# A list-scheduled kernel gets a new order, three new constants in its planner, and two units of q whose exponentials run row by row

## The chip, the cores and the metric

One Trainium2 chip, one core. The metric is the device time of one execution in microseconds (us), as the median of repeated runs. A profiled execution, recorded separately, gives the rows shown below.

## The reference

Three layers follow one another, all in float32. Linear attention comes first (4 batches, 8 heads, 576 positions, 64 columns): a softmax of q over its columns, a softmax of k over the positions, and `q_s @ (k_s^T @ v)`. Its result, 2304 x 512, passes through a SwiGLU layer and then a bilinear one.

```python
q_s = np.exp(q - q.max(-1)); q_s /= q_s.sum(-1) + 1e-9      # row by row
k_s = np.exp(k - k.max(2));  k_s /= k_s.sum(2) + 1e-9       # column by column
x = einsum('bhsd,bhde->bhse', q_s, einsum('bhsd,bhse->bhde', k_s, v))
x = (silu(x @ w_gate) * (x @ w_val)) @ w_out                # 512 -> 1536 -> 512
x = (x @ w_a) * (x @ w_b) @ w_out2                          # 512 -> 1536 -> 512
```

## The kernel before, in words

**Precision.** Each operand of the large products is split into a high part and a low part (float32r), and a product is three passes of TensorE: low by high, high by low, high by high. Cutting the operands apart is work of VectorE, ScalarE and GpSimd. The weights arrive in a wide format of two 32-bit words per number, and are converted first: for a tile of w_gate, w_val and w_out (`convert`, lines 367 to 452) the steps are an absolute value (L421 on ScalarE or L423 on VectorE), a scaling of the low words (L426, ScalarE), two clamps and shifts (L428, L431, VectorE), a merge of signs (L437, VectorE), an addition of the low words (L442, VectorE or GpSimd), the high part (L447, ScalarE) and the low part (L331, the helper `pair`, VectorE or GpSimd). Tile f of layer 1 is called `w_f`; a tile has 1536 columns, and from tile 4 on it comes in two halves of 768.

**Stages.** The attention of a batch has four units of two heads (`attend`, from L536). A unit takes its largest k (`tm`, `kx`, `kr`, `kb`), the exponentials, `kv` (L745), the normalised and transposed q (`qt`, `ql`), and at the end `xt` and `xl` (L809, L819), whose result for batch 0 is split into `xhl`, the input of the first up products. A unit's buffers are called `ut` (units of batches 0 and 1). Then block 0 of layer 1 runs over twelve weight tiles: products `u_0_f` (L860 for f = 0, L875 later), gate and product on ScalarE and VectorE (`s`, L886, L889), splitting into `h`, and down products `acc` (L902) of the tile before. Block 1 does the same, with the attention of batches 2 and 3 between its products. From about 265 us on, the rest of layer 1 and the whole of layer 2 run as 18 steps of a Strassen-like scheme (products `p`, `q`, `o`, from L1154), with sums and splits (`raww`, `l2w`, `temps`, `latewr`) on VectorE, ScalarE and GpSimd.

**What sets the order.** Every operation is given to a `Plan` (L31) with its engine, an estimated cost, what it reads and writes, and for some of them a second engine that could do it. `Plan.prepare` works out a due time for each, backwards from the products; `emit` adds the corrections of the table `MOVES` (number of the operation, shift in us) and `order` then simulates the engines and picks, again and again, the ready operation of earliest due time. The instructions are issued in that order: each engine's queue is fixed when the kernel is built, and an engine that waits holds back all that stands behind it. The constants `HOP`, `FROM_TENSOR`, `DMA_RATE` and `DMA_END` exist only in this simulation; on the chip they matter by the order that comes out.

**The q exponentials.** In the units of batch 0 GpSimd subtracts a row's maximum from q (L709, L713), one ACTIVATE takes the exponential of k and q together (1280 columns, L717), and VectorE adds up the rows (L768). In the units of the other batches the maximum is given as the bias of nine ACTIVATEs on ScalarE, one for each row group, which also return the row's sum (L728); k has its own exponential of 640 columns (L721). The tuple `BYROW` names the units of batch 0 that take the second way; before it is empty.

Of the kernel before, what the change touches and what calls it, by code (L numbers as in the profile page):

```python
# [30 lines left out]
class Plan:  # L31
# [10 lines left out]
    SAME, HOP, TO_TENSOR, TO_GPSIMD, FROM_TENSOR = 0.033, 0.1, 0.055, 0.1, 0.2  # L42
    OVER = dict(vector=0.08, scalar=0.1, gpsimd=0.045)
    PORT = 0.08
    SLACK = 0.7
    DMA_START, DMA_END, DMA_RATE, DMA_LANES = 1.0, 1.45, 330e3, 8
# [25 lines left out]
    def add(self, engine, cost, fn, reads=(), writes=(), due=None, after=(), table=None, nbytes=0, other=None,  # L72
# [3 lines left out]
        for access, write in [(a, False) for a in reads] + [(a, True) for a in writes]:  # L76
# [14 lines left out]
            for key, (last, readers) in buf.seen.items():  # L91
                if part is None or key is None or key == part:
                    if last is not None:
                        deps.add(last)
                    if write:
                        deps.update(readers)
# [1295 lines left out]
```

## Time and profile before

| | |
|---|---|
| median of 3 runs | 938.73 us (938.71 to 941.14) |
| the profiled execution | 938.23 us |
| its span, first to last instruction | 936.4 us |
| TensorE busy | 901.8 us, 96% of the span |
| VectorE, ScalarE, GpSimd busy | 69%, 57%, 37% |
| DMA | 121.45 MB, 130 GB/s over the span |

A busy TensorE is one with a matmul under way; matmuls overlap, so that the mean duration of one in a list is longer than the step from one to the next. The profiled execution lies 0.5 us below the median of the runs, and its span 1.8 us below its own time.

### The profile page before, as it was taken

Reading aid. Unit: us, or ns where it says so; the run is one execution under the profiler, and the core shown is the slowest. Engines: PE = TensorE matmul, PEld = TensorE weight load, DVE = VectorE, ACT = ScalarE, POOL = GpSimd, SP = SyncE. Lnnn points to the kernel's source line nnn. Section 1 sums busy time; section 2 is a strip of 40 time slices with the busy share of each in tenths; the row PEclk is TensorE's granted clock in tenths of the full one; section 3 lists DMA queues with packets and bytes.
Section 4 is the critical chain, followed back from the end, with each engine's and each line's share of the span. In section 5 each row is a group of like instructions: output and inputs, shape, how many; then the busy total and the mean of one; then the engine's idle time right before and its main releaser. Section 6 shows DMA issues by size and latency. Waiting matters only on the chain.

```text
span 936.4 us, 13123 instructions
## 1 busy us (share of the span) xinstructions
PE 901.8 (96%) x4560; PEld 742.4 (79%) x4560; DVE 646.6 (69%) x1025; ACT 529.4 (57%) x1027; POOL 347.5 (37%) x324
## 2 busy tenths in 40 slices
PE   5599999999999999999999999999999999999998
PEld 3377777777787888888887888888878888788886
DVE  7899996553498898676778778765686444454444
ACT  4999987868566665555462556443543453333310
POOL 6523212112063233444574534662765213242210
PEclk9999999999999999999999999999999999999999
DMA  9968874453437455454413664422032210110003
GB/s 270 292 215 245 274 231 157 136 179 110 115 108 239 138 164 186 143 155 128 132 57 101 214 203 122 122 84 67 23 98 84 79 46 23 45 45 23 23 1 113
DMA packets 108154, 121.45 MB, mean 130 GB/s; under 512 B 31928, under 2 KB 83896, under 8 KB 107960
## 3 DMA queue, kind: packets, MB, share of 16 engines
q1 hardware_dynamic: 102424, 116.55, 40.0%
q10 hardware_dynamic: 5664, 4.07, 1.3%
q8 instruction: 36, 0.59, 0.3%
q14 instruction: 30, 0.25, 0.1%
HBM read 88.60 MB, written 31.98 MB: 129 GB/s over the span
## 4 chain that ended last, share of the span: by engine, by line
PE 78%; DVE 12%; DMA 4%; issue 2%; ACT 1%; SPq 1%; DVEq 0%; ACTq 0%
PE p L1154 33%; PE o L1264 15%; PE u L875 8%; PE q L1238 7%; PE o L1266 6%; PE acc L902 4%; PE o L1273 2%; DVE a L437 2%; DVE w L331 1%; DVE a L442 1%; DVE l2w L331 1%; DVE a L428 1%; PE xt L809 1%; DVE a L431 1%; DMA latewr<-in_moe_w_out_dram 1%
## 5 line engine op out<-in xcount | busy, mean ns | idle before, releaser
L1154 PE MATMUL p<-l2w,l2w 128*128 128x512 f32 x1512 | 353.1, 390 | 1.6 <-DVE temps L331 1.6
L1154 PEld LDWEIGHTS p<-l2w,l2w 128*128 128x128 f32 x1512 | 282.8, 188 | 62.1 <-DVE temps L331 2.9
L875 PE MATMUL u<-xhl,w 128*128 128x512 f32 x552 | 142.5, 405 | 4.9 <-POOL w L331 2.8
L331 POOL TENSOR_TENSOR l2w<-raww,l2w 128x512 fp32r<-128x512 f32 x71 | 106.0, 1496 | 87.1 <-ACT l2w L338 84.7
L338 ACT CAST l2w<-raww 128x512 fp32r<-128x512 f32 x144 | 88.2, 621 | 81.9 <-PE p L1154 37.7
L875 PEld LDWEIGHTS u<-xhl,w 128*128 128x128 f32 x552 | 101.4, 191 | 29.5 <-DVE w L331 4.8
L331 DVE TENSOR_TENSOR sums<-o,sums 128x512 f32<-128x512 f32 x120 | 82.4, 688 | 53.6 <-PE o L1264 40.7
L331 DVE TENSOR_TENSOR temps<-p,temps 128x512 f32<-128x512 f32 x90 | 61.9, 688 | 54.0 <-PE p L1154 52.7
L1264 PE MATMUL o<-l2w,hp 128*128 128x512 f32 x288 | 97.0, 391 | 0.9 <-DVE sums L331 0.9
L331 DVE TENSOR_TENSOR l2w<-raww,l2w 128x512 fp32r<-128x512 f32 x73 | 57.5, 799 | 29.9 <-ACT l2w L338 29.8
L1166 ACT COPY temps<-p 128x512 f32<-128x512 f32 x72 | 42.1, 586 | 60.6 <-PE p L1154 58.6
L902 PE MATMUL acc<-h,w 128*128 128x512 f32 x288 | 73.0, 399 | 0.0
L507 POOL TENSOR_TENSOR latewr<-latewr 128x512 uint32<-128x512 uint32 x23 | 33.0, 1437 | 93.1 <-DVE latewr L502 87.1
L1238 PE MATMUL q<-rest,l2w 128*128 128x256 f32 x432 | 65.4, 283 | 0.0
L1264 PE MATMUL o<-l2w 128*128 128x512 f32 x192 | 64.4, 389 | 0.0
L1264 PEld LDWEIGHTS o<-l2w,hp 128*128 128x128 f32 x288 | 53.3, 188 | 13.3 <-DVE sums L331 2.8
L902 PEld LDWEIGHTS acc<-h,w 128*128 128x128 f32 x288 | 53.1, 188 | 12.4 <-issue 1.4
L1238 PEld LDWEIGHTS q<-rest,l2w 128*128 128x128 f32 x432 | 58.6, 192 | 0.9
L331 POOL TENSOR_TENSOR raww<-raww,spare 128x512 f32<-128x512 f32 x12 | 17.3, 1442 | 89.1 <-DVE l2w L331 88.9
L1266 PE MATMUL o<-hp,l2w 128*128 128x512 f32 x144 | 48.7, 392 | 1.1 <-DVE sums L331 1.1
L1264 PE MATMUL o<-l2w,l2w 128*128 128x512 f32 x168 | 49.7, 390 | 0.0
L1266 PE MATMUL o<-l2w 128*128 128x512 f32 x144 | 48.3, 390 | 0.0
(192 smaller groups left out, 1463.3 us busy)
## 6 DMA issues: line engine op xcount, KB each, us to landing
raww<-wf SPq DMA_DIRECT2D x36, 512.0 KB, 3.8
raww<-wf SPq DMA_DIRECT2D x36, 256.0 KB, 3.2
wf<-latewr SPq DMA_DIRECT2D x36, 256.0 KB, 3.4
wf<-a SPq DMA_DIRECT2D x16, 384.0 KB, 2.7
latewr<-in_moe_w_a_dram SPq DMA_DIRECT2D x24, 256.0 KB, 4.2
latewr<-in_moe_w_b_dram SPq DMA_DIRECT2D x24, 256.0 KB, 3.1
latewr<-in_moe_w_out_dram SPq DMA_DIRECT2D x12, 512.0 KB, 5.1
wr<-in_moe_w_gate_dram SPq DMA_DIRECT2D x22, 256.0 KB, 4.0
```

Source lines behind the costliest of these rows:

```text
L331: engine.tensor_tensor(out=out(), in0=x(), in1=y(), op=op)
L338: add("scalar", act_us(n), lambda: nc.scalar.copy(out=hi(), in_=src()), src_keys, [hi_key])
L437: add("vector", dve_us(e), lambda rows=rows, halves=halves: nc.vector.scalar_tensor_tensor(out=a(halves), in0=rows()[..., 1], scalar=0xC00 ...
L507: engine.tensor_tensor(out=u32(), in0=u32(), in1=r()[..., 0], op=ALU.add)
L875: nc.tensor.matmul(ps()[:, 0:n], lhsT=wv[:, c, :], rhs=x()[:, xs, c, 0:n], start=(a == 0 and c == 0), stop=(a == 2 and c == KD - 1))
L902: nc.tensor.matmul(ps()[:, 0:n], lhsT=w()[:, 4 + ws, o * P:(o + 1) * P], rhs=h()[:, hs, 0:n], start=begin, stop=end)
L1154: nc.tensor.matmul(ps()[:, 0:width], lhsT=wv(o)[:, m, ws, c, :], rhs=ops_x[o][xs][1]().rearrange("p (c n) -> p c n", c=2)[:, c, 0:width], ...
L1166: add("scalar", act_us(n), lambda: nc.scalar.copy(out=to[1]()[:, 0:n], in_=ps()[:, 0:n]), [ps], [to[0]], due=main["at"] + main["soon"])
L1238: nc.tensor.matmul(ps[m]()[:, 0:256], lhsT=wv(o)[:, m, ws, c % 2, :], rhs=rest_x[xs][1]().rearrange("p (c n) -> p c n", c=KD)[:, c, :], st ...
L1264: nc.tensor.matmul(ps(), lhsT=lhs(i, hs), rhs=outs_w[i][1]()[:, ws * 512:(ws + 1) * 512], **ends)
L1266: nc.tensor.matmul(ps()[:, 0:width], lhsT=outs_w[i][1]()[:, ws * 512 + r * P:ws * 512 + (r + 1) * P], rhs=hs2[i][t][1]()[:, hs * 512:hs * ...
L1273: nc.tensor.matmul(ps()[:, o * 256:(o + 1) * 256], lhsT=outs_w[i][1]()[:, ws * 512 + at:ws * 512 + at + P], rhs=rest_h[1]()[:, (2 * i + hs ...
```

## The change

Four constants or rules of the simulation are new: the rate of the DMA queues is taken as 345 KB/us (330 before), the landing as 1.4 us (1.45); a place that a matmul only read counts as free 0.04 us before that product's end (`READ_BY_TENSOR`), where 0.2 us was added before for any dependency on TensorE; and a slot is free 0.033 us after its last user (0.1 before). `MOVES` is a wholly new table. `BYROW` becomes (1, 3): two of the four units of batch 0 take their exponentials of q row by row.

```diff
+    READ_BY_TENSOR = -0.04
...
-    DMA_START, DMA_END, DMA_RATE, DMA_LANES = 1.0, 1.45, 330e3, 8
+    DMA_START, DMA_END, DMA_RATE, DMA_LANES = 1.0, 1.4, 345e3, 8
...
-        27, 38.5, 35, -20.2, 47, -5.8, 52, -11.1, 53, 7.6, 79, -9.5, 88, -3.9, 93, -18.9, 100, -28.2, 119,
...
+        3, 17.6, 6, 34.4, 8, 13, 9, 39.6, 39, 18.8, 44, 21.6, 53, -48.3, 57, 2.5, 60, 29.3, 70, -26.4, 71,
...
                     if last is not None:
                         deps.add(last)
+                        made.add(last)
...
-    def hop(self, first, then):
+    def hop(self, first, then, made=True):
 
         if first == "tensor":
-            return 0.0 if then == "tensor" else self.FROM_TENSOR
+            return 0.0 if then == "tensor" else self.FROM_TENSOR if made else self.READ_BY_TENSOR
...
-            return max(end[u] for u in users) + self.HOP if all(u in end for u in users) else self.FAR
+            if not all(u in end for u in users):
+                return self.FAR
+            return max(end[u] + (self.READ_BY_TENSOR if ops[u]["engine"] == "tensor" else self.SAME) for u in users)
...
-    BYROW = ()
+    BYROW = (1,3)
```

The file grows by nine lines: L331 of before is L340 after it, L442 is L451, L860 is L869.

**TensorE, start of the SwiGLU layer.** Before, all four units of batch 0 are finished when the first products `u_0_0` begin, and between them and those of tile 1 (`u_0_1`) stand the first products of a unit of batch 1 (`kx_483`, `kb_496`):

```order
L860 MATMUL u_0_0_0_410<-xhl_0_304,w_0_347 128x512 x3
L860 MATMUL u_0_0_1_420<-xhl_0_304,w_0_347 128x512 x3
L680 MATMUL kx_483<-ident,tm_477 128x128 x2
L680 MATMUL kx_483<-ident,ut_425 128x128
L685 MATMUL kb_496<-ident,kr_492 128x128
L875 MATMUL u_0_1_0_513<-xhl_0_304,w_1_475 128x512 x12
L875 MATMUL u_0_1_1_557<-xhl_0_304,w_1_475 128x512 x12
L902 MATMUL acc_0_581<-h_0_0_508,w_0_347 128x512 x3
```

Now the first chunk of `u_0_0` stands ahead of the end of the third unit (`ut_103`) and the fourth (`ut_106`), and nothing stands between `u_0_0` and `u_0_1`:

```order
L805 MATMUL qt_367<-ident,ut_103 128x128 x4
L869 MATMUL u_0_0_0_376<-xhl_0_339,w_0_254 128x512 x3
L808 MATMUL ql_397<-ident_87,ut_103 128x64
L818 MATMUL xt_400<-ut_103 128x512
L828 MATMUL xl_412<-ut_103 128x64
L869 MATMUL u_0_0_1_415<-xhl_0_339,w_0_254 128x512 x3
L869 MATMUL u_0_0_0_376<-xhl_0_339,w_0_254 128x512 x3
L869 MATMUL u_0_0_1_415<-xhl_0_339,w_0_254 128x512 x3
L805 MATMUL qt_432<-ident,ut_106 128x128 x4
L869 MATMUL u_0_0_0_376<-xhl_0_339,w_0_254 128x512 x3
```

The first products of batch 1 have moved behind `u_0_1`, into the down products.

**VectorE, weight tile 1.** Before, the two last splits of `xhl` and the chain of tile 1 (`a_1`) end with the addition L442, and the split of `w_1` is not in this queue:

```order
L442 ISA a_0_1_255<-wr_0_1_169,a_0_1_255 128x1024
L331 TENSOR_TENSOR xhl_0_304<-xt_388,xhl_0_304 128x512
L428 TENSOR_SCALAR a_1_0_402<-a_1_0_402 128x1536
L331 TENSOR_TENSOR xhl_0_304<-xt_398,xhl_0_304 128x512
L431 TENSOR_SCALAR a_1_0_402<-a_1_0_402 128x1536
L437 SCALAR_TENSOR_TENSOR a_1_0_402<-wr_1_223,a_1_0_402 128x1536
L428 TENSOR_SCALAR a_0_2_456<-a_0_2_456 128x512
L442 ISA a_1_0_402<-wr_1_223,a_1_0_402 128x3072
L431 TENSOR_SCALAR a_0_2_456<-a_0_2_456 128x512
```

Now the chain is followed by the last of `xhl`, three steps of tile 0's third part (`a_0_2`) and the split of `w_1` itself:

```order
L340 TENSOR_TENSOR xhl_0_339<-xt_400,xhl_0_339 128x512
L446 SCALAR_TENSOR_TENSOR a_1_0_381<-wr_1_223,a_1_0_381 128x1536
L451 ISA a_1_0_381<-wr_1_223,a_1_0_381 128x3072
L340 TENSOR_TENSOR xhl_0_339<-xt_453,xhl_0_339 128x512
L437 TENSOR_SCALAR a_0_2_441<-a_0_2_441 128x512
L440 TENSOR_SCALAR a_0_2_441<-a_0_2_441 128x512
L446 SCALAR_TENSOR_TENSOR a_0_2_441<-wr_0_2_215,a_0_2_441 128x512
L340 TENSOR_TENSOR w_1_463<-a_1_0_381,w_1_463 128x2x3x256
L711 TENSOR_REDUCE st_491<-ut_429 128x8
```

The split of `w_1` came to this queue, with the absolute value of the tile ahead of it (it was on ScalarE).

**GpSimd, the same place.** Before, the addition L442 for `a_0_2` and then the split of `w_1`:

```order
L660 MEMSET ut_425 64x64 x4
L663 MEMSET ut_425 128x9
L442 TENSOR_TENSOR a_0_2_456<-a_0_2_456,wr_0_2_218 128x512
L331 TENSOR_TENSOR w_1_475<-a_1_0_402,w_1_475 128x2x3x256
L698 MEMSET ut_425 128x128
L660 MEMSET ut_511 64x64 x2
```

Now the split of tile 0's third part, and no work for tile 1:

```order
L669 MEMSET ut_429 64x64 x4
L672 MEMSET ut_429 128x9
L451 TENSOR_TENSOR a_0_2_441<-a_0_2_441,wr_0_2_215 128x512
L340 TENSOR_TENSOR w_0_254<-a_0_2_441,w_0_254 128x512
L669 MEMSET ut_518 64x64 x4
L672 MEMSET ut_518 128x9
L793 TENSOR_TENSOR ut_429<-ut_429,st_491 128x512
```

The split of `w_1` has left this queue. Over the whole program ScalarE has 34 loads of its function tables where it had 40 (16 where it had 22 up to the last weight tile of layer 1), and GpSimd has 214 of the two-operand instructions where it had 221; on TensorE the order from the first of the 18 steps on is the same.

## Rows read from the trace of the kernel before

**Rows 1.** Page, part 1: busy us (share of span) xinstructions.

```profile
PE 901.8 (96%) x4560; PEld 742.4 (79%) x4560; DVE 646.6 (69%) x1025; ACT 529.4 (57%) x1027; POOL 347.5 (37%) x324
```

**Rows 2.** Windows of 20 us: length, busy us per engine (x), PEclk, DMA share, GB/s.

```profile
0.00:20.00 20.00, 8.93 (x64) 5.86 (x65) 14.05 (x33) 7.51 (x16) 12.60 (x26) 1.00 0.90 256
20.00:40.00 20.00, 14.34 (x98) 9.83 (x96) 17.00 (x32) 18.35 (x31) 10.07 (x15) 1.00 0.94 306
40.00:60.00 20.00, 14.57 (x74) 11.18 (x75) 18.85 (x27) 19.54 (x39) 8.19 (x10) 0.83 0.74 239
...
140.00:160.00 20.00, 18.50 (x82) 14.54 (x81) 13.91 (x21) 14.83 (x36) 4.44 (x12) 1.00 0.53 171
...
300.00:320.00 20.00, 19.91 (x110) 17.49 (x111) 17.60 (x29) 12.76 (x25) 7.73 (x5) 1.00 0.49 148
```

**Rows 3.** Timeline, TensorE: start, us, engine, line, out<-in, count, [idle before <-releaser].

```profile
32.35 5.72 PE L860 MATMUL u<-xhl,w 128*128 128x512 f32 x24
41.69 0.44 PE L680 MATMUL kx<-ident,tm 128*128 128x128 f32 x2 [3.62 <-DVE tm L331]
...
46.23 7.30 PE L875 MATMUL u<-xhl,w 128*128 128x512 f32 x24 [2.76 <-POOL w L331]
...
55.50 0.80 PE L745 MATMUL kv<-ut 128*64 128x65 f32 x20
...
57.78 3.92 PE L875 MATMUL u<-xhl,w 128*128 128x512 f32 x16 [0.20 <-DVE w L331]
```

**Rows 4.** Windows of 2 us around TensorE's slow stretch (columns as in rows 2).

```profile
40.00:42.00 2.00, 0.32 (x3) 0.32 (x3) 2.00 (x5) 1.98 (x3) 0.62 (x1) 1.00 0.73 295
42.00:44.00 2.00, 0.68 (x4) 0.18 (x1) 1.37 (x4) 1.99 (x4) 2.00 (x2) 0.70 0.86 199
...
48.00:50.00 2.00, 2.00 (x7) 1.53 (x7) 1.97 (x2) 2.00 (x13) 0.00 (x0) 0.59 1.06 375
```

**Rows 5.** Timeline, VectorE (columns as in rows 3).

```profile
32.00 0.69 DVE L331 TENSOR_TENSOR xhl<-xt,xhl 128x512 fp32r<-128x512 f32 x1 [1.66 <-ACT xhl L338]
...
38.01 1.75 DVE L442 CUSTOM_DVE_ANT_0 a<-wr,a 128x3072 uint16<-128x3072 uint16 x1
...
44.88 2.34 DVE L428 TENSOR_SCALAR a<-a 128x1536 f32<-128x1536 f32 x1 [0.49 <-ACT a L421]
...
55.98 1.75 DVE L331 TENSOR_TENSOR w<-a,w 128x1536 fp32r<-128x1536 f32 x1
```

**Rows 6.** Timeline, GpSimd.

```profile
42.73 3.44 POOL L331 TENSOR_TENSOR w<-a,w 128x1536 fp32r<-128x1536 f32 x1
```

**Rows 7.** Timeline, ScalarE.

```profile
10.47 1.27 ACT L717 ACTIVATE ut<-ut 128x1280 f32<-128x1280 f32 x1 [1.09 <-POOL ut L713]
...
41.62 1.28 ACT L728 ACT_TABLE_LOAD   x1
...
49.47 0.36 ACT L728 ACTIVATE ut<-ut,st 128x64 f32<-128x64 f32 x1
...
49.80 0.36 ACT L728 ACTIVATE ut<-ut,st 128x64 f32<-128x64 f32 x1
...
50.47 0.73 ACT L721 ACTIVATE ut<-ut 128x640 f32<-128x640 f32 x1
```

**Rows 8.** Groups by shape, 0 to 160 us: busy us, mean ns | idle before.

```profile
L728 ACT ACT_TABLE_LOAD x10 | 12.8, 1283 | 0.2
...
L768 DVE TENSOR_REDUCE st<-ut 128x10 f32<-128x640 f32 x4 | 3.2, 810 | 0.2 <-ACT ut L717 0.2
...
L756 DVE TENSOR_SCALAR ut<-kv,ks 64x64 f32<-64x64 f32 x10 | 2.8, 280 | 0.4 <-DVE a L431 0.2
```

**Rows 9.** Timeline, TensorE after 60 us, rows with idle before them.

```profile
148.85 5.30 PE L875 MATMUL u<-xhl,w 128*128 128x512 f32 x22 [1.50 <-DVE w L331]
...
327.19 1.66 PE L1154 MATMUL p<-l2w,l2w 128*128 128x512 f32 x6 [0.61 <-DVE temps L331]
```

**Rows 10.** Timeline, VectorE, end of the last weight tile's conversion.

```profile
144.25 2.62 DVE L442 CUSTOM_DVE_ANT_0 a<-wr,a 128x1536 uint16<-128x1536 uint16 x1
```

More of the change, by code (lines that the diff above doesn't have):

```diff
@@ L74, in add @@
         n = len(self.ops)
-        deps, order, allocs = set(), set(after) | set(hold), []
+        deps, order, allocs, made = set(), set(after) | set(hold), [], set()
         for access, write in [(a, False) for a in reads] + [(a, True) for a in writes]:
@@ L105, in add @@
         self.ops.append(dict(engine=engine, cost=cost, runs=runs, deps=deps, order=order - deps, wanted=due,
-                             allocs=allocs, table=table, nbytes=nbytes, hold=hold))
+                             allocs=allocs, table=table, nbytes=nbytes, hold=hold, made=made))
         return n
-    def hop(self, first, then):
+    def hop(self, first, then, made=True):
         if first == "tensor":
-            return 0.0 if then == "tensor" else self.FROM_TENSOR
+            return 0.0 if then == "tensor" else self.FROM_TENSOR if made else self.READ_BY_TENSOR
         return dict(gpsimd=self.TO_GPSIMD, tensor=self.TO_TENSOR).get(then, self.SAME)
@@ L232, in order @@
                     at = ops[s]["engine"]
-                    is_ready(s, max([end[d] + self.hop(ops[d]["runs"][run[d]][0], at)
+                    is_ready(s, max([end[d] + self.hop(ops[d]["runs"][run[d]][0], at, d in ops[s]["made"])
                                      for d in ops[s]["deps"]] + [issued[d] for d in ops[s]["order"]]))
```

35 rows, old and new, of the table MOVES are left out of this document.

## The prediction

> **What bounds the kernel now.** The page first: TensorE is busy 901.8 us of a span of 936.4 us, far ahead of the other engines [rows 1]. So no rearrangement can win more than the 34.6 us in which TensorE has no matmul, and what it spends at a lower clock. The windows come next, since an average says nothing of where those 34.6 us lie. In the first three windows TensorE works 8.93, 14.34 and 14.57 us of 20, which leaves 22.2 us idle in the first 60 us [rows 2]; after that a window lacks a microsecond or two at most, and the rows of TensorE with the largest waits show 1.50 us at 148.85 us and 0.61 us at 327.19 us [rows 9]. The change can therefore pay in one place: the way from the first load to the dense stream, which begins with the products of tile 2 at 57.78 us.
>
> In that stretch the engines' queues set the pace. VectorE works 18.85 us of the third window and ScalarE 19.54 us [rows 2]. TensorE finishes `u_0_0` at 38.07 us, then waits 3.62 us for VectorE, and begins `u_0_1` only at 46.23 us, released by GpSimd [rows 3]: the split of `w_1` ran there for 3.44 us, to 46.17 us [rows 6]. While TensorE sat idle its granted clock fell (0.70 of full as the mean of 42 to 44 us), and it was back in the window from 48 to 50 us [rows 4]. The 24 matmuls of `u_0_1` took 7.30 us, the 24 of `u_0_0` before them 5.72 us [rows 3]: 1.6 us are lost to the clock.
>
> **The change part by part.** The work of TensorE is the same; I follow when its next operand is ready. The sum is made against the profiled execution's 938.23 us and then set on the median, 0.5 us above it.
>
> *Tile 1's chain on VectorE, up to the addition.* Before, it ends at 38.01 + 1.75 = 39.76 us [rows 5]. Up to the same step the new queue has four more scalings of `kv` (0.28 us each [rows 8], which ScalarE did) and the absolute value of tile 1; it loses the row sums of units 1 and 3 (0.81 us each [rows 8]) and the last split of `xhl` (0.69 us by [rows 5]). VectorE has no 1536-wide absolute value in the trace. The step L428 of that width is the nearest row, and it has 2.34 us beside GpSimd's 3.44 us [rows 5, 6]; the steps of that chain that read two inputs take 1.75 us [rows 5]. One with one input, alone, I put at 1.0 us, between half of 1.75 and 2.34. The other steps that came and went are of like shapes and cancel within 0.2 us. Together 1.1 + 1.0 - 1.6 - 0.7 - 0.2 = -0.4 us of work. The wait of 1.66 us for `xhl` [rows 5] should go, since the chain of tile 1 now begins ahead of that split, and with it some 0.8 us of the wait for the absolute value, which VectorE now makes itself. Against that I charge 0.5 us for the absolute value of tile 0, which now stands early in VectorE's queue, ahead of the subtractions of k: if the tile lands late, the attention waits behind it. That gives 39.8 - 0.4 - 2.5 + 0.5 = 37.4 us, with bounds of 36.5 us (no such wait, less stretching) and 39.8 us (all waits remain in other places).
>
> *Tile 1 ready.* Behind the addition stand one `xhl` split, three short steps of tile 0 and the split of `w_1`, 0.7 + 1.4 + 1.75 us less their overlaps: 40.9 us. Before it was 46.17 us. That is 5.3 us earlier at `u_0_1`. The first products of batch 1, 1.1 us, which TensorE made in its idle time before, now come later, behind `u_0_1`.
>
> *Tile 2 ready.* Here most of it is given back, because VectorE has taken work from the others. From the end of tile 1's addition to the end of `w_2`'s split before were 57.73 - 39.76 = 18.0 us [rows 5]. In that stretch VectorE gets the split of `w_1` (1.75), the absolute value of tile 2 (1.0), one `xhl` split (0.7) and a short step (0.4); it hands on a split to GpSimd and passes three steps of later work behind `w_2` (2.8 us together, by the same widths). It loses the 0.49 us of waiting and the 1.4 us by which the clamp of 2.34 us was stretched [rows 5]. 18.0 + 3.85 - 2.8 - 1.9 = 17.1 us, so `w_2` comes at 54.5 us. TensorE needs it earlier: 40.9 us plus 5.6 us for `u_0_1`, 2.8 us for `acc` and 1.2 us for small products is 50.5 us. A new wait of 4 us stands where 0.20 us stood [rows 3]. `u_0_2` begins 3.3 us earlier than before, but the `kv` of batch 1 (0.80 us [rows 3]) is still to do: 2.4 us are left. The 1.6 us of slow clock are inside this figure.
>
> *Tiles 3 to 11.* Until the last tile both engines are nearly full, so TensorE cannot run ahead of VectorE. For tile 3 VectorE needs about 10.4 us more (64.9 us), TensorE is there at 64.3 us: 0.6 us given back. At the end of the tiles the addition took 2.62 us beside GpSimd [rows 10], where half of a 1.75 us step is 0.9 us. GpSimd's split of that tile is now on VectorE (0.9 us more), so some 0.8 us of the 1.50 us wait [rows 9] can go; I take 0.5 us. ScalarE loses six table loads of 1.28 us [rows 7, 8], 7.7 us, which covers the later split casts but ends no wait by itself.
>
> *The row-wise exponentials.* An ACTIVATE with its sum follows the next in 0.33 us (49.47 to 49.80 us [rows 7]), so nine take about 3.0 us. The exponential of 1280 columns (1.27 us) shrinks to 640 (0.73 us) [rows 7]. Two units cost ScalarE 5 us more. ScalarE is busy only 7.51 us of the first 20 us [rows 2], where those of unit 1 stand, and I cost them at nothing; those of unit 3 stand in the second window (18.35 us busy), and if that cover is gone the last `xhl` is up to 2.5 us late. GpSimd's two subtractions per unit go.
>
> *After tile 11.* On TensorE the order of the 18 steps is the same. I cost it at nothing.
>
> Sum: -2.4 + 0.6 - 0.5 = **-2.3 us**. 938.23 - 2.3 is 935.9 us for a profile, and 936.4 us against the median of 938.73 us: a gain of 0.25%. A measurement of this kernel can tell about 0.3%, 2.8 us, from no change.
>
> **A rule against it.** The new wait of 4 us before `u_0_2` is of the size of the wait after `u_0_0`, behind which the granted clock fell to 1.2 GHz with 0.32 us of matmul work in 40 to 42 us [rows 4]. In the new wait stand small products, so I let the clock stay. The Trainium skill, in TensorE: Matmul & The Clock Gate, "What's actually happening", holds that the slow state is the default and that only activity lifts it. By that rule the loss of 1.6 us returns at `u_0_2`, and the sum would be -0.7 us.
>
> **The rivals.**
> - *The lead of tile 1 is kept.* If VectorE is less stretched by GpSimd than before, so that `w_2` is ready near 51.5 us, TensorE hardly waits, and 3 us more stay: 933.4 us. For it speaks that GpSimd no longer runs the 3.44 us split [rows 6]; against it VectorE's full windows [rows 2].
> - *Given back whole.* The clock falls again, or `xhl` and the chain keep all their waits (39.8 us instead of 37.4 us for the addition): -2.3 + 1.6 or + 2.4, about 938.5 us.
> - *Slower.* VectorE takes over instructions from GpSimd also in the 18 steps, where it is busy 17.6 us of 20 in the window from 300 us [rows 2]. Each time a sum of `temps` comes too late TensorE waits, 0.61 us at 327.19 us [rows 9]. Ten more such waits are 6.1 us: 938.7 - 2.3 + 6.1 = 942.5 us. It decides from about nine waits on (5.1 us) to be slower by what can be told. Against it: VectorE's share falls in the later steps.
> - That the change does nothing is excluded by the queues, which differ from the first microseconds on.
>
> **How the numbers follow.** The forecast has 0.46: 936.4 us with 934.6 to 938.2 us as its own range, of which 0.18 is faster by over 0.3% and 0.28 within it. The kept lead has 0.20, all faster. Given back has 0.22, all within 0.3%. Slower has 0.12. That makes 0.38, 0.50 and 0.12. The range from 932.0 to 940.5 us leaves out most of the slower case and the tail of the kept lead.
>
> **What would show it.** Right: `u_0_1` begins near 41 us and not behind GpSimd; a wait of 3 to 5 us for `w_2` on VectorE before `u_0_2`, which begins near 54.5 us; idle of TensorE in the first 60 us near 21 us; a granted clock of 1.00 from 40 to 60 us. Wrong: `u_0_1` later than 43 us, `u_0_2` before 52 us or after 57 us, or waits of TensorE beyond 150 us that add up to over 5 us.

## The result, and the profile after

The changed kernel takes 945.84 us (median of five runs, 944.83 to 948.17) against 938.73 us (five runs, 938.70 to 941.14): a ratio of 1.0074 with a 95% interval of 1.0061 to 1.0087, so 7.1 us slower. The forecast of 936.4 us and its range up to 940.5 us are missed on the slower side. The profiled execution took 946.55 us, its span is 944.6 us. The page of the changed kernel, part 1, answers to [rows 1]:

```profile
PE 909.1 (96%) x4560; PEld 743.7 (79%) x4560; DVE 656.2 (69%) x1043; ACT 520.6 (55%) x1051; POOL 318.4 (34%) x308
```

The number of matmuls is the same, yet TensorE is busy 7.3 us longer, and its idle time grew by 0.9 us only, to 35.5 us. A busy TensorE that gets no more done is one that runs at a lower clock or one whose matmuls wait inside their busy time. GpSimd has 29 us less to do and VectorE 10 us more. The windows of 20 us (columns as in [rows 2]) say where:

```profile
0.00:20.00 20.00, 8.96 (x45) 5.95 (x45) 13.48 (x33) 9.83 (x33) 9.45 (x22) 1.00 0.89 245
20.00:40.00 20.00, 14.77 (x103) 10.57 (x103) 18.59 (x33) 14.27 (x38) 11.28 (x16) 0.83 0.90 301
40.00:60.00 20.00, 14.86 (x58) 10.70 (x57) 17.04 (x22) 18.33 (x37) 7.27 (x9) 0.91 0.75 236
```

ScalarE does 4.1 us less between 20 and 40 us than before, GpSimd 3.2 us less in the first 20, and the granted clock falls twice, not once. TensorE's timeline (columns as in [rows 3]):

```profile
28.02 0.94 PE L869 MATMUL u<-xhl,w 128*128 128x512 f32 x3
32.36 0.66 PE L808 MATMUL ql<-ident,ut 128*128 128x64 f32 x2 [3.40 <-DVE ut L765]
...
34.91 3.94 PE L869 MATMUL u<-xhl,w 128*128 128x512 f32 x9
38.69 0.60 PE L805 MATMUL qt<-ident,ut 128*128 128x128 f32 x4
...
47.25 2.17 PE L884 MATMUL u<-xhl,w 128*128 128x512 f32 x7 [2.88 <-ACT s L895]
...
60.13 0.32 PE L694 MATMUL kb<-ident,kr 128*128 128x128 f32 x1 [1.27 <-ACT ut L812]
60.39 0.96 PE L884 MATMUL u<-xhl,w 128*128 128x512 f32 x3
```

The new order starts `u_0_0` while the attention of units 2 and 3 is still under way: three matmuls at 28.02 us, then a wait of 3.40 us, then nine more matmuls, and only behind them, at 38.69 us, the turning of unit 3's q. `u_0_1` begins at 47.25 us, 1.0 us later than before [rows 3], and `u_0_2` at 60.39 us, 2.6 us later. Windows of 2 us around the slow stretches:

```profile
30.00:32.00 2.00, 0.00 (x0) 0.00 (x0) 1.88 (x7) 1.82 (x3) 1.64 (x3) 0.90 1.08 390
32.00:34.00 2.00, 1.64 (x4) 1.15 (x5) 1.94 (x3) 0.44 (x3) 1.94 (x3) 0.50 1.08 389
...
36.00:38.00 2.00, 2.00 (x6) 1.56 (x5) 1.97 (x3) 1.60 (x2) 0.00 (x0) 0.50 0.33 96
...
50.00:52.00 2.00, 2.00 (x6) 1.51 (x5) 1.73 (x3) 2.00 (x3) 1.96 (x3) 0.50 1.04 304
```

After 3.40 us without a matmul the clock is at 1.2 GHz (0.50) while the nine matmuls run: 3.94 us, where a run below that keeps the clock up takes 2.33 us for the same nine. It falls again behind the idle ahead of `u_0_1`. VectorE's timeline shows what became of tile 1 (to be set against [rows 5]):

```profile
37.88 1.76 DVE L451 CUSTOM_DVE_ANT_0 a<-wr,a 128x3072 uint16<-128x3072 uint16 x1
42.20 0.69 DVE L340 TENSOR_TENSOR xhl<-xt,xhl 128x512 fp32r<-128x512 f32 x1 [2.56 <-ACT xhl L347]
...
44.34 1.75 DVE L340 TENSOR_TENSOR w<-a,w 128x1536 fp32r<-128x1536 f32 x1
...
58.59 1.75 DVE L340 TENSOR_TENSOR w<-a,w 128x1536 fp32r<-128x1536 f32 x1
```

Tile 1's addition ends at 39.64 us (39.76 before). Up to it VectorE was busy longer than before, and idle less (windows, columns as in [rows 2], before and after):

```profile
0.00:39.76 39.76, 23.27 (x160) 15.69 (x160) 30.81 (x64) 25.62 (x46) 22.67 (x40) 1.00 0.93 283
```

```profile
0.00:39.64 39.64, 23.36 (x145) 16.21 (x146) 32.07 (x65) 23.83 (x70) 20.73 (x37) 0.91 0.90 273
```

Behind the addition VectorE stands still for 2.56 us, because the last `xhl` comes so late, and the split of `w_1` is done at 46.09 us: it has moved from GpSimd to VectorE [rows 6] and ends at the same moment. From there, by starts and ends in the timelines:

| us | before | after | later by |
|---|---|---|---|
| `w_1` ready | 46.17 | 46.09 | -0.1 |
| `u_0_1` begins | 46.23 | 47.25 | 1.0 |
| `w_2` ready | 57.73 | 60.34 | 2.6 |
| `w_5` ready | 86.53 | 92.83 | 6.3 |
| `w_11` ready | 148.80 | 153.32 | 4.5 |
| first product of the 18 steps | 282.7 | 288.0 | 5.3 |
| first `q` of the second step | 331.4 | 336.5 | 5.1 |
| last matmul ends | 931.8 | 940.0 | 8.2 |

So there are two losses in this profile: 6 us up to `w_5`, of which about 1 us is back by 330 us, and 3 us behind that.

One profile is one execution. Six of the runs below (s_old_steps, g_old_steps, steps_engines, steps_act, steps_dve and steps_actdve) have the changed kernel's own order up to the first product of the 18 steps. In their profiles `w_1` is ready between 42.8 and 45.7 us, `w_11` between 150.8 and 153.8 us, and the first product comes between 284.2 and 288.3 us. A difference of a microsecond or two between two profiles therefore says little by itself, and what an edit is worth is read from the ratios of the runs.

### The profile page after: what moved, and what is told of

The parts are those of the page before. It is cut to its first block, busy times and chain, and to the rows that moved or that the text cites. A ratio compares the mean times of both kernels' runs of the same rounds, so it can differ in the third digit from the quotient of the medians.

```text
span 944.6 us, 13120 instructions
## 1 busy us (share of the span) xinstructions
PE 909.1 (96%) x4560; PEld 743.7 (79%) x4560; DVE 656.2 (69%) x1043; ACT 520.6 (55%) x1051; POOL 318.4 (34%) x308
## 3 DMA queue, kind: packets, MB, share of 16 engines
q1 hardware_dynamic: 102424, 116.55, 39.8%
## 4 chain that ended last, share of the span: by engine, by line
PE 75%; DVE 10%; DMA 5%; ACT 3%; issue 3%; SPq 2%; POOL 0%; DVEq 0%; ACTq 0%; POOLq 0%
PE p L1163 32%; PE o L1273 14%; PE u L884 7%; PE q L1247 7%; PE o L1275 7%; PE acc L911 3%; PE o L1282 2%; DMA wr<-in_moe_w_out_dram 1%; DVE a L446 1%; DVE w L340 1%; DMA uq<-in_q_dram 1%; PE xt L818 1%; DVE l2w L340 1%; DVE a L451 1%; SPq L640 1%
## 5 line engine op out<-in xcount | busy, mean ns | idle before, releaser
L1163 PE MATMUL p<-l2w,l2w 128*128 128x512 f32 x1512 | 357.1, 391 | 2.2 <-ACT temps L1175 1.0
L340 POOL TENSOR_TENSOR l2w<-raww,l2w 128x512 fp32r<-128x512 f32 x69 | 97.2, 1410 | 211.4 <-ACT l2w L347 204.6
L340 DVE TENSOR_TENSOR sums<-o,sums 128x512 f32<-128x512 f32 x120 | 82.6, 689 | 59.8 <-PE o L1273 42.3
L340 DVE TENSOR_TENSOR temps<-p,temps 128x512 f32<-128x512 f32 x90 | 62.0, 688 | 51.5 <-PE p L1163 49.1
L340 DVE TENSOR_TENSOR l2w<-raww,l2w 128x512 fp32r<-128x512 f32 x75 | 59.3, 799 | 21.7 <-ACT l2w L347 21.6
L516 POOL TENSOR_TENSOR latewr<-latewr 128x512 uint32<-128x512 uint32 x17 | 24.2, 1424 | 76.3 <-DVE latewr L511 73.1
L1273 PEld LDWEIGHTS o<-l2w 128*128 128x128 f32 x192 | 36.0, 188 | 7.6
```

The lines of the kernel that those rows point to most:

```text
L340: engine.tensor_tensor(out=out(), in0=x(), in1=y(), op=op)
L516: engine.tensor_tensor(out=u32(), in0=u32(), in1=r()[..., 0], op=ALU.add)
L1163: nc.tensor.matmul(ps()[:, 0:width], lhsT=wv(o)[:, m, ws, c, :], rhs=ops_x[o][xs][1]().rearrange("p (c n) -> p c n", c=2)[:, c, 0:width], ...
L1273: nc.tensor.matmul(ps(), lhsT=lhs(i, hs), rhs=outs_w[i][1]()[:, ws * 512:(ws + 1) * 512], **ends)
```

## The experiments

In the experiments on the order the planner's choice is replaced by a list of the operations, each with its engine, its place and the buffer that it takes, and the list is then changed. All else is the kernel's own code:

```diff
     def emit(self):
-        self.prepare()
...
-        done, run, slot = self.order()
+        pending = [*self.LISTED, 0]
+        for x, y in zip(pending, pending[1:]):
...
```

A ratio below is to runs of the kernel before on the same chip.

**Which half?** The first two runs join the orders at the first product of the 18 steps.

```diff
# s_old_start
+LISTED: before up to p0_0_0, changed behind it
# s_old_steps
+LISTED: changed up to p0_0_0, before behind it
```

> The order of the kernel before up to the first product of the 18 steps (its unit exponentials too), the changed kernel's order from there on, written out as a list. Theory (two thirds of the loss arise before 90 us, where u_0_0 is woven into the attention of units 2 and 3; one third is spread over the 18 steps): the start is as fast as before and only the steps lose their 2.7 us, about 941.4 us. Rival 1 (the steps only look slower, because their queues start late): 938.7 us, no change. Rival 2 (the steps alone are the cause and the start catches up): 945 us or more.

> The reverse: the changed kernel's order up to the first product of the 18 steps, from there on the order of the kernel before. Theory: the first product of the steps still comes 5.3 us late, the steps run at the old pace, about 943.9 us. Rival 1 (the steps lose only what the start hands on): 945.8 us, as the changed kernel. Rival 2: 939 us.

Measured: 947.40 us, 1.0090 (1.0070 to 1.0110), and 944.73 us, 1.0053 (1.0034 to 1.0072). The first is slower than the change itself. The traces show why the two prove nothing: from the first product to the first `q` they took 26.6 and 24.2 us, in their two parents 20.2 and 20.3 us. At the seam the two orders hold different PSUM banks (the places that take TensorE's sums). That the crossed banks are what delayed the products was not tested by itself, for the next two runs move the seam as well, to a place where both orders have issued the same operations, and rename the banks:

```diff
# g_old_steps
+LISTED: changed up to q1_0_0, before behind it; at0->acc2, acc2->acc3, acc3->at0
# g_old_start
+LISTED: before up to q1_0_0, changed behind it; at0->acc3, acc3->acc2, acc2->at0
```

> The changed kernel's order up to the small products q of the second of the 18 steps; from there on the order of the kernel before, with the PSUM banks renamed so that each goes on with the bank that is free (the two first trials changed order at the first product and left the banks crossed, which cost 4 to 6 us between the first product and q). By the trace the changed kernel loses 3.1 us behind this place (536.9 before, 540.0 after, from q of step 2 to the last product's end region). Theory (the steps lose 3 us of their own, by ScalarE's and VectorE's order): 945.8 - 3 = about 942.8 us. Rival (a late start is handed on and the steps lose nothing themselves): 945.8 us.

> The reverse: the order of the kernel before up to the same place, the changed kernel's order behind it, banks renamed. Theory: 938.7 + 3 = about 941.7 us. Rival: 938.7 us.

Measured: 942.28 us, 1.0043 (1.0030 to 1.0055), and 940.61 us, 1.0024 (1.0012 to 1.0037). The new start alone costs 4.0 us, the new steps alone 2.3 us. Together that is 6.3 of the 7.1 us, and the rest lies within the intervals. Both rivals fall: the steps lose time of their own.

**Row-wise exponentials.**

```diff
# r_rows_alone: the order before
-    BYROW = ()
+    BYROW = (1,3)
# r_rows_undone: the changed order
-    BYROW = (1,3)
+    BYROW = ()
```

> One part of the change alone: the order of the kernel before, with the exponentials of q taken row by row on ScalarE in units 1 and 3, which stand where the joint exponential stood; GpSimd's subtractions and VectorE's sums of these units are gone. Theory (the order is the cause, the ScalarE work is covered): within 1.5 us of 938.7 us. Rival (5 us more of ScalarE delay unit 3, the last xhl and with it u_0_1): 941 to 944 us, u_0_1 2 to 5 us later than at 46.2 us.

> The changed kernel's order with the joint exponential of units 1 and 3 put back (subtractions by GpSimd, exponential and sums in the place of the row-wise ones). Theory: within 1.5 us of 945.8 us, the waits of TensorE at 28 to 36 us and 44 to 47 us stay. Rival (the row-wise exponentials are the cause): 939 to 941 us.

Measured: 942.05 us, 1.0037 (1.0024 to 1.0049), and 948.72 us, 1.0099 (1.0081 to 1.0116). ScalarE of r_rows_alone, the end of unit 3's exponentials and the splits of `xhl` behind them:

```profile
27.42 0.40 ACT L945 ACTIVATE ut<-rests,st 128x128 f32<-128x128 f32 x1
...
27.80 0.57 ACT L555 CAST xhl<-xt 128x512 fp32r<-128x512 f32 x1
...
36.91 0.61 ACT L555 CAST xhl<-xt 128x512 fp32r<-128x512 f32 x1
```

The same two casts of the kernel before:

```profile
23.93 0.59 ACT L338 CAST xhl<-xt 128x512 fp32r<-128x512 f32 x1
...
33.42 0.64 ACT L338 CAST xhl<-xt 128x512 fp32r<-128x512 f32 x1
```

The second `xhl` comes 3.9 us later, the last one 3.5 us later, `u_0_1` begins 3.4 us later (49.66 us), and 3.5 us of it are there at the end: the rival was right for the old order. In the new order the joint exponential is no cure: with it the run is 2.3 us slower still by the ratios (the two intervals overlap a little). I put GpSimd's subtractions directly ahead of the exponential in that list, which may be a bad place for them, so this run says nothing of the exponentials in an order made for them. So the exponentials cost what the order around them lets them cost.

**The start: unit 3's place, the clock, VectorE's work.** In unit3_first TensorE's queue reads (`-` as in the changed kernel):

```diff
 MATMUL xl<-ut 128x64
+MATMUL qt<-ident,ut 128x128 x4
 MATMUL u_0_0_1<-xhl_0,w_0 128x512 x3
 MATMUL u_0_0_0<-xhl_0,w_0 128x512 x3
+MATMUL xt<-ut 128x512
 MATMUL u_0_0_1<-xhl_0,w_0 128x512 x3
-MATMUL qt<-ident,ut 128x128 x4
...
-MATMUL xt<-ut 128x512
```

> The changed kernel's order with one thing moved: unit 3's turning products, its copy on ScalarE, its attention product and the split behind it stand ahead of the second and later chunks of u_0_0 and ahead of the scaling of wr_2, not behind them. Theory A (queues: u_0_0 woven into the attention makes the last split of xhl come 4 us late, and tile 1 behind it): the last xhl on VectorE at about 38 us instead of 42.2, u_0_1 at 44 instead of 47.3 us, and 2 to 4 us less in all, about 943 us. Theory B (from 46 to 150 us VectorE's preparation of the tiles sets the pace, 98% busy in both kernels): what counts is VectorE's wait of 2.56 us before the last xhl; it goes, and the end comes at most 2.5 us earlier; with VectorE as full as before. If neither the wait nor u_0_1 matters: 945.8 us.

In clock_fill the first three products of `u_0_0` are made six times:

```diff
-                    for a, (ws, xs) in enumerate(((1, 0), (0, 1), (0, 0))):
+                    for a, (ws, xs) in enumerate(((1, 0), (0, 1), (0, 0)) * (6 if (c, m) == (0, 0) else 1)):
...
```

> The changed kernel's order with 15 more products on TensorE that repeat u_0_0's first three (the sums stay what they are), put where it waits from 28.9 to 32.4 us. Theory C (the clock: the idle lets the granted clock fall to 0.5 from 32 to 38 us, which doubles 6 us of products): the clock stays at 1.00 there, the last xhl comes 3 us earlier and the end 2 to 3 us, about 943 us. Theory B (VectorE sets the pace): only what VectorE's own wait before the last xhl loses comes back, at most 2.5 us. Theory A (queues alone): within 1 us of 945.8 us, as the chunks still stand ahead of unit 3.

vector_less leaves out one VectorE instruction, the clamp, in each tile or half tile of the tiles 2 to 5:

```diff
# vector_less
-        add("vector", dve_us(size, 2), lambda: nc.vector.tensor_scalar(
+        add("vector", dve_us(size, 2), lambda: (l == 0 and 2 <= f <= 5) or nc.vector.tensor_scalar(
```

> The changed kernel's order; the clamp of the magnitudes (one VectorE instruction per tile or half tile) is left out for the tiles 2 to 5 of the first layer, so 4 us of VectorE's work between 48 and 90 us are gone and nothing else is. Theory B (VectorE sets the pace from tile 1 to tile 11): every later tile is ready up to 4 us earlier and the end comes 3 to 4 us earlier, 942 to 943 us. Theories A and C (the start before 48 us is the cause, TensorE is the bound behind it): within 1 us of 945.8 us.

Measured: unit3_first 944.25 us, 1.0067 (1.0052 to 1.0082); clock_fill 943.60 us, 1.0057 (1.0042 to 1.0072); vector_less 942.88 us, 1.0051 (1.0035 to 1.0068), all beside 1.0074 for the change. unit3_first is not told from the change. The wait at the last `xhl` shrank from 2.56 to 0.38 us, but a new one, for ScalarE's absolute value, stands right behind that split:

```profile
41.06 0.43 DVE L645 TENSOR_SCALAR a<-a 128x512 f32<-128x512 f32 x1 [1.33 <-ACT a L638]
```

`w_1` was ready at 44.34 us, but of these 1.75 us some 1.0 us stand ahead of the edit, since `u_0_0` already began at 27.04 us. `u_0_1` still waited for ScalarE, to 46.09 us, and `w_11` came at 153.29 us as before the edit. Theory A is at most a small part. clock_fill gives 1.6 us by the ratios, but its interval overlaps that of the change, so the run alone does not make even the sign sure; its windows of 2 us have no slow stretch left at 32 to 38 us:

```profile
32.00:34.00 2.00, 2.00 (x10) 1.39 (x10) 1.97 (x2) 1.26 (x5) 1.93 (x4) 1.00 1.08 389
...
36.00:38.00 2.00, 2.00 (x9) 1.30 (x8) 1.97 (x2) 0.51 (x1) 0.00 (x0) 1.00 0.56 177
```

and its TensorE:

```profile
27.43 4.37 PE L1077 MATMUL u<-xhl,w 128*128 128x512 f32 x18
...
33.12 2.33 PE L1077 MATMUL u<-xhl,w 128*128 128x512 f32 x9
```

Its `w_1` is ready at 42.67 us (3.4 us earlier, of which 0.6 us stand ahead of the edit), `w_11` at 150.73 us (2.6 us earlier). A second witness is the profile of steps_act, a run of the last experiment, whose order is the change's own up to 330 us. Behind the same wait, with no product added, its clock stayed at 1.00 from 28 to 42 us:

```profile
31.94 0.41 PE L1016 MATMUL ql<-ident,ut 128*128 128x64 f32 x2 [3.43 <-DVE ut L973]
...
33.24 2.32 PE L1077 MATMUL u<-xhl,w 128*128 128x512 f32 x9
```

There `w_1` is ready at 42.79 us and `w_11` at 150.77 us, as in clock_fill. In the change's own profile and the five others of this order the clock fell to 0.50 behind this wait; there `w_1` came between 44.6 and 46.1 us and `w_11` between 152.0 and 153.8 us. Against the profile of steps_act the fall costs 1 to 3 us at `w_11`, and it does not happen in every execution. That is theory C, for a part of the loss.

vector_less takes 4.1 us from VectorE's work up to tile 11 (135.1 us busy, 139.2 in the change) and gains 2.2 us at the end by the ratios, again with overlapping intervals. Its `w_11` comes 2.3 us earlier, but its `w_1`, which the edit does not reach, is 1.4 us earlier too. From `w_1` to `w_11` it takes 106.3 us, where the seven profiles of the change's order take 107.0 to 108.1 us. So 0.7 to 1.8 of the 4.1 us arrive at `w_11`. VectorE sets the pace there for a part, and not alone: theory B is true for a part of the loss. The windows up to `w_1` and from there to `w_11` show VectorE's share. Before:

```profile
0.00:46.20 46.20, 24.26 (x164) 16.18 (x164) 36.14 (x73) 31.67 (x53) 27.50 (x43) 0.96 0.91 280
46.20:148.80 102.60, 98.98 (x494) 76.82 (x494) 98.24 (x152) 95.48 (x177) 25.35 (x39) 0.98 0.72 236
```

After:

```profile
0.00:46.10 46.10, 27.48 (x160) 18.76 (x160) 35.90 (x71) 28.60 (x76) 22.28 (x38) 0.93 0.88 268
46.10:153.30 107.20, 98.82 (x498) 77.12 (x498) 103.27 (x155) 92.14 (x181) 30.17 (x42) 0.98 0.72 231
```

Up to `w_1` all three helpers have done less in the same time, ScalarE 3.1 and GpSimd 5.2 us. From `w_1` to `w_11` VectorE is 96% busy in both kernels (ScalarE 93% before and 86% after), and in the changed one it has 5.0 us more to do. The stretch is 4.6 us longer.

**Is it the start or the middle?**

```diff
# m_new_start
+LISTED: changed up to u0_0_1, before behind it
# m_new_middle
+LISTED: before up to u0_0_1, changed up to u0_0_11, before behind it
```

> The changed kernel's order only up to the first product of u_0_1 (47 us; u_0_0 woven into the attention, row-wise exponentials, tile 1 on VectorE), from there on the order of the kernel before. Theory 1 (idle, clock and in-order waits before 47 us are the larger part): 941 to 943 us. Theory 2 (it is the order from 47 to 150 us, which gives VectorE more work and puts attention ahead of tiles): 938 to 940.5 us.

> The order of the kernel before up to u_0_1 (46 us), the changed kernel's from u_0_1 to u_0_11 (47 to 150 us), that of the kernel before again behind it. Theory 1: within 1 us of 938.7 us. Theory 2: 941 to 943 us, with the tiles 2 to 5 ready 4 to 6 us later against tile 1 than in the kernel before (w_5 40.4 us behind w_1 there, 46.7 us in the changed kernel).

Measured: 945.51 us, 1.0069 (1.0045 to 1.0093), and 939.17 us, 1.0005 (0.9993 to 1.0016). Theory 2 falls: the new order from 47 to 150 us, put behind the old start, costs nothing that can be told. VectorE needs 134.7 us up to `w_11` there, as in the kernel before (134.4). In m_new_start, with the old middle, it needs 137.7 us, and in the change 139.2 us. The additional work is therefore for the larger part what the new start leaves undone or loads on VectorE, not a trait of the middle. m_new_start even overshoots the 4.0 us of g_old_steps: `w_1` at 45.23 us is followed by `w_2` at 62.68 us, 17.5 us instead of 11.6, since the old middle expects the first work on unit 4 to be done. So its number is an upper bound of the start's cost.

**Tile 1 on VectorE, and a busy TensorE, in the kernel before.**

```diff
# before_w1_vector, at the place behind kr of unit 4
-GpSimd:  TENSOR_TENSOR w_1<-a_1_0,w_1 128x2x3x256
+VectorE: TENSOR_TENSOR w_1<-a_1_0,w_1 128x2x3x256
# before_busy: the same, and
+                again(34 if x == 0 else 0), nc.tensor.transpose(ps()[:, x * P:(x + 1) * P], part(), ident)),
...
+        add("tensor", 0.13, lambda: (nc.tensor.transpose(pb(), kr().to_broadcast([P, P]), ident), again(24)), [kr], [pb])
```

> The kernel before with one part of the change alone: the third split of tile 1 (w_1) stands on VectorE instead of GpSimd, between the maximum kr and the subtractions of unit 4. By the prediction's step: w_1 ready at about 44.6 us instead of 46.2, u_0_1 1.6 us earlier, the end 0 to 1.6 us earlier. Theory B: u_0_1 is earlier, but VectorE has 1.75 us more in its queue (and saves 1.4 us, the stretch of the instruction that ran beside GpSimd's split), so tile 2 and the end come no earlier, within 1 us of 938.7 us.

> The kernel before with tile 1's third split on VectorE (as in before_w1_vector) and TensorE kept busy in its two waits between u_0_0 and u_0_1 by 58 transposes whose result is the one that stands there already (unit 4's remainder of k). If the clock before tile 2 costs anything: it stays at 1.00 from 40 to 52 us and the end comes 1 to 1.7 us earlier than 938.3 us, which would beat both kernels. If tile 2 is the bound (57 us): u_0_1 ends earlier, TensorE waits longer for w_2, and the end stays within 0.8 us of 938.3 us.

Measured: before_w1_vector 937.83 us, 1.0000 (0.9983 to 1.0017): `w_1` 1.7 and `u_0_1` 1.7 us earlier (44.54 us), `w_2` 1.0 us earlier, nothing at the end. before_busy 941.42 us, 1.0035 (1.0022 to 1.0047), slower, which neither expectation had. Its TensorE and VectorE:

```profile
46.45 5.72 PE L1087 MATMUL u<-xhl,w 128*128 128x512 f32 x24
```

```profile
43.08 0.56 DVE L895 TENSOR_REDUCE kr<-kx 128x1 f32<-128x384 f32 x1 [1.18 <-PE kx L892]
...
46.73 0.29 DVE L538 TENSOR_TENSOR ut<-ut,kb 128x128 f32<-128x128 f32 x1 [0.83 <-PE kx L888]
```

The products `u_0_1` of before_w1_vector, to set against the first row:

```profile
44.54 7.93 PE L1082 MATMUL u<-xhl,w 128*128 128x512 f32 x24 [1.13 <-DVE w L538]
```

The clock is at 1.00 from 40 to 54 us, and the 24 matmuls of `u_0_1` take 5.72 instead of 7.93 us. But the transposes made VectorE wait 1.18 + 0.83 us, and `u_0_1` began 1.9 us later than in before_w1_vector, so that it ended only 0.3 us earlier. `w_2` came 1.65 us later (58.41 against 56.76 us), and the end 3.3 us later by the ratios. So the run does not tell what a faster `u_0_1` alone would be worth. It goes with before_w1_vector, where `u_0_1` 1.7 us earlier was worth nothing, and shows that filling TensorE's wait costs more than it gives where VectorE has to wait for it.

**All repairs together.**

```diff
# combo
+LISTED: changed with unit3_first up to q1_0_0, before behind it; with clock_fill
```

> The changed kernel's order with three repairs at once: unit 3 ahead of the later chunks of u_0_0 (as in unit3_first), the 15 repeated products in TensorE's first long wait (as in clock_fill), and the order of the kernel before from q of step 2 on (as in g_old_steps). If the three parts are separate they add up: 945.8 - 1.0 - 1.9 - 3.6 = about 939.3 us. If unit 3 and the clock are one and the same loss (the wait before unit 3 is what lets the clock fall): 940.5 to 941 us.

Measured: 940.16 us, 1.0013 (0.9996 to 1.0030). Against g_old_steps (1.0043) unit 3's place and the clock are worth 2.8 us together, the old steps were worth 2.9 us (1.0074 to 1.0043). What is left of the loss is 1.2 us, and cannot be told from none. Whether unit 3's place and the clock are one loss or two stays open, since 940.16 us lies between the two expectations. It beats the change and not the kernel before; no version that I ran beats both.

**The 18 steps.** The view of the waits (us in total, times, longest) from 330 us on, TensorE's weight loads and one row of ScalarE, in the kernel before:

```profile
PEld o L1264 <- DVE sums L331: 2.8, 5, 0.7
PEld o L1266 <- DVE sums L331: 2.3, 3, 1.2
PEld p L1154 <- DVE temps L331: 0.6, 1, 0.6
PEld p L1154 <- ACT temps L1166: 0.6, 2, 0.3
...
ACT l2w L338 <- DVE raww L331: 5.8, 6, 3.2
```

After:

```profile
PEld p L1163 <- ACT temps L1175: 4.7, 14, 0.9
PEld p L1163 <- ACT p L1201: 2.4, 5, 0.7
PEld o L1273 <- DVE sums L340: 1.4, 3, 0.6
PEld o L1275 <- DVE sums L340: 1.1, 1, 1.1
...
ACT l2w L347 <- DVE raww L340: 20.9, 8, 3.1
```

The products now wait 7.1 us for ScalarE's copies, where it was 0.6 us; the waits for sums fell from 5.1 to 2.5 us. ScalarE itself waits 20.9 us for VectorE's differences of raw weights, 5.8 us before. One place of ScalarE's timeline, where a scaling of late weights waits and a copy behind it comes late (TensorE waited 0.47 us for it, at 408.36 us):

```profile
406.66 0.66 ACT L504 ACTIVATE latewr<-latewr 128x512 uint32<-128x512 uint32 x1 [1.26 <-DVE latewr L511]
407.22 0.62 ACT L1179 ACTIVATE temps<-temps 128x512 f32<-128x512 f32 x1
407.75 0.56 ACT L1175 COPY temps<-p 128x512 f32<-128x512 f32 x1
```

Is it the engines or the order?

```diff
# behind q1_0_0 of the changed list
+steps_engines: 91 operations back on the engine they had before
+steps_act: ScalarE's operations in the order they had before
+steps_dve: VectorE's operations in the order they had before
+steps_actdve: both
```

> The changed kernel's order; behind q of step 2 each of the 91 instructions that the change gave to another engine goes back to the engine of the kernel before, at its place in the changed order. Theory (the steps lose because differences of the raw weights went from GpSimd to VectorE, so casts and conversions on ScalarE wait for VectorE and the copies of TensorE's results stand behind them): 942.5 to 944 us, and TensorE's weight loads wait less for ScalarE than 7.6 us. Rival (it is the order on ScalarE itself, whatever the engines): within 1 us of 945.8 us or slower.

> The changed kernel; behind q of step 2 only ScalarE's queue goes back to the order of the kernel before (179 of its instructions move, by at most 7 places; 25 on VectorE move with them), each on the engine that the change gave it. Theory (copies of TensorE's results stand on ScalarE behind casts and conversions that wait): about 943 us, and the weight loads of the products wait less for ScalarE than 7.6 us. Rival (VectorE's order is the cause, ScalarE only waits for it): 945.8 us or slower.

> The changed kernel; behind q of step 2 only VectorE's queue goes back to the order of the kernel before (220 of its instructions move, by at most 14 places). Theory (ScalarE's own order): 945.8 us or slower. Rival (VectorE's order): about 943 us.

> Both queues in the order of the kernel before behind q of step 2, the engines those of the change. If order is the whole loss of the steps: 942.3 us, as with all of the order before. If order and engines only work together, as the run with the old engines in the new order suggests: 945 us or slower.

Measured: 952.85 us, 1.0153 (1.0134 to 1.0171); 947.85 us, 1.0099 (1.0082 to 1.0115); 966.09 us, 1.0293 (1.0273 to 1.0313); 962.88 us, 1.0266 (1.0240 to 1.0293). None comes near the 942 to 944 us of the theory, and each ratio is above that of the change (for steps_act the two intervals just overlap), so the theory falls in each of its forms. steps_act did what was said of ScalarE, its waits of the same view fell, and VectorE's took their place:

```profile
PEld p L1371 <- DVE temps L548: 4.4, 4, 3.0
PEld o L1483 <- DVE sums L548: 4.4, 4, 2.0
PEld p L1371 <- ACT temps L1383: 1.9, 4, 0.6
```

Which operations of the steps cost the 2.3 us stays open. Shown is that neither the old engines alone nor the old order of ScalarE's and VectorE's queues brings it back, and that here half of an order mixed with half of another is worse than either. GpSimd's queue was not put back by itself.

## Why the prediction was wrong

**"Tile 1's chain on VectorE, up to the addition"** was put at 37.4 us with bounds of 36.5 to 39.8 us; it came at 39.64 us. The waits ahead of it did shrink: that for `xhl` from 1.66 to 0.60 us, and VectorE's whole idle time up to the addition by 1.4 us, where 2.0 us were put. What failed here is the work, put at -0.4 us: VectorE was busy 32.07 us against 30.81 us, 1.3 us more. With every instruction counted at the shortest of its shape in these two stretches, I estimate the work itself at 0.3 us less, much as it was put. The rest is instructions that ran longer while GpSimd was at work, and for more of that than before I had put nothing.

**"Tile 1 ready"** was put at 40.9 us; it was 46.09 us. 2.2 of these 5.2 us were there at the addition, and 2.56 us are the wait for the last `xhl` behind it. The step that failed is "the wait of 1.66 us for `xhl` should go", with no wait put behind the addition. I counted VectorE's own instructions and left out that the operand of the last `xhl` depends on TensorE's queue, where `u_0_0` now stands ahead of unit 3's `qt`. The wait came back behind the addition, longer than it had been. `u_0_1` was also not free to begin: it waited for ScalarE's `s`, which I had not walked. The sentence "wrong: `u_0_1` later than 43 us" has come true with 47.25 us.

**"Tile 2 ready"** was put 13.6 us behind tile 1; it came 14.3 us behind (60.34 us). This term was sized nearly right, but it stood on a start 5.2 us too early. That VectorE pays for what it takes over is the part of the working that held: with the split of `w_1` on VectorE alone `u_0_1` began 1.7 us earlier and nothing of it reached the end (before_w1_vector), as "most of it is given back" had it.

**"Tiles 3 to 11"** were to give back 0.6 us and win 0.5 us. From `w_2` to `w_11` 1.9 us more were lost (2.6 to 4.5 us late).

**"I let the clock stay"** was wrong. I looked for the idle ahead of `u_0_2`, while it arose at 28.96 and 44.38 us. The Trainium skill, in TensorE: Matmul & The Clock Gate, "What's actually happening", has the slow state as the default, and the trace agrees: 0.50 granted from 32 to 38 us and from 50 to 52 us, behind 3.40 and 2.88 us without a matmul. Keeping the clock up in the first of the two gave 1.6 us by the ratios of clock_fill, with overlapping intervals. That this is the figure I had named for the rule against is luck, since it arose at another place and on another path: the slower matmuls stand ahead of unit 3's `qt` and make the last `xhl` late. In steps_act the same wait of 3.43 us left the clock at 1.00, so the loss is not there in every execution.

**"The row-wise exponentials ... I cost them at nothing"** was wrong for the old order, where they cost 3.5 us (r_rows_alone), with the last `xhl` 3.5 us late against the "up to 2.5 us" that I named for the case that the cover is gone. The cover was judged by ScalarE's share in windows of 20 us; what counts is what stands behind the nine instructions. What they cost in the new order, of which the forecast spoke, no run tells.

**"After tile 11 ... I cost it at nothing"** was wrong by 2.3 us (g_old_start). I had compared TensorE's order alone and found it the same. The slower rival named this place and took VectorE's sums of `temps` as the mechanism, at 0.6 us each for ten waits. There is a loss there, but it is less than half as large, the waits are for ScalarE's copies, and putting the engines back makes it worse, so its mechanism is not confirmed.

**The sum.** I had -2.4 us up to tile 2, +0.6 and -0.5 us for tiles 3 to 11, 0 for the steps. Measured by the joined orders are +4.0 us for the start and +2.3 us for the steps. The second sign of failure that I named, `u_0_2` after 57 us, is there too (60.39 us).

## What to carry to other kernels

Where every engine's queue is fixed ahead, follow one operand through all queues that it passes, TensorE's included, before a wait is struck from the sum: a wait that one engine loses often stands one instruction later on the next. Find the engine that is full in the stretch (here VectorE, 96% from tile 1 to tile 11) and price each idle or added microsecond of it, without taking for granted that all of it arrives: 4.1 us less work gave 2.2 us. An earlier start of TensorE's products there was worth nothing (before_w1_vector). An order and its choice of engines belong together: take a part of one over into another only at a seam where both have issued the same work and hold the same buffers.

## What the runs showed of the hardware

A VectorE instruction over nine columns took 1.25 us beside a GpSimd split of 512 columns; the same instruction took 0.17 us at 54.24 us, with GpSimd idle. VectorE of the changed kernel:

```profile
30.01 1.25 DVE L782 TENSOR_SCALAR st<-st 128x9 f32<-128x9 f32 x1
...
54.24 0.17 DVE L782 TENSOR_SCALAR st<-st 128x9 f32<-128x9 f32 x1 [0.39 <-ACT ut L737]
```

GpSimd of the changed kernel:

```profile
29.35 1.87 POOL L340 TENSOR_TENSOR w<-a,w 128x512 fp32r<-128x512 f32 x1 [2.95 <-ACT w L456]
```

The short instruction ends at 31.26 us, GpSimd's at 31.22 us: it ran to the end of it. The Trainium skill, in SBUF — State Buffer, "SBUF: two separate sides", has the port pair that the two engines share as a lock held for a whole instruction; for VectorE it names instructions in a two-port mode or with two inputs in SBUF. The two ends agree with such a lock, while no row shows the mode of the short instruction. I had priced such stretching for long instructions only. This short one stands in VectorE's queue ahead of the scalings of `kv` (L765) for which TensorE waited 3.40 us.

The 58 transposes of 128 columns in before_busy held the granted clock at 1.00 through an idle in which it had fallen to 0.50 before, and behind 15 repeated products in clock_fill it stayed at 1.00 too. But a wait of the same length does not always let it fall: behind 3.40 us without a matmul it went to 0.50 in the change, and behind 3.43 us, in the same order, it stayed at 1.00 in steps_act. Behind 2.88 us, ahead of `u_0_1`, it went to 0.50 in the change, and behind 2.87 us it stayed at 1.00 in steps_dve and steps_engines.
